# An attention kernel with routed experts: where weight quarters are loaded, and when the first transposes are copied

## The chip, the cores and the metric

The kernel runs on one core of one Trainium2 chip. That core has five instruction streams that work side by side: TensorE (PE, with its weight loads PEld), VectorE (DVE), ScalarE (ACT), GpSimd (POOL) and SyncE (SP). POOL and SP issue the DMAs here. The metric is the time of one execution in microseconds on the device, as the median of several runs.

## The reference

Attention over 8 sequences of 576 tokens with 8 heads of 64, with a position bias that is the same for all sequences, and then one of 8 expert networks for each token:

```python
scores = scale * np.matmul(q, k.transpose(0, 1, 3, 2))
x = (np.log1p(np.abs(rel)) / psi_i)[..., None]
bias = np.maximum(x @ w1 + b1, 0.0) @ w2
scores = scores + bias.transpose(2, 0, 1)[None]
attn = softmax(scores)
attn_out = np.matmul(attn, v)                 # 8 x 8 x 576 x 64
x = attn_out as (4608 tokens, 512)
for e in range(8):
    mask = domain_id == e
    out[mask] = np.maximum(x[mask] @ w1[e], 0.0) @ w2[e]   # 512 -> 1024 -> 512
```

## The kernel before

**Bias.** `_phase_bias` computes the bias once, in nine blocks `ib` of positions. `hidden` makes 16 rows `hr` for a block on VectorE (L202) and ScalarE (L199); `outputs` multiplies them on TensorE in three groups (chunks 0 and 1, chunks 2 and 3, chunk 4), each into one of three score buffers of the ring `G.ring()`. ScalarE writes exp(bias) from there (L234, L237, L244), and for chunk 3 VectorE also takes a raw copy from the same buffer (`biasW`, L241). `hidden(ib + 1)` is issued ahead of `outputs(ib)`. The bias code is a generator: it stops at each `yield`, and `run` calls it again at chosen units (`LAST_ROWS`), so that the three groups of block 8 lie between the first scores.

**Attention.** `_Attention.run` goes through the sequences b = 0 to 7 in an order written out by hand (`ROUND`). A unit such as `m01` is the scores of head pair 0 and key chunk 1: two matmuls (L532) into a ring buffer, and an exp on ScalarE (L560, tile `e`). `r` units are for the 64 last keys, `l` and `x` for the 64 last queries. `W` multiplies with the bias on VectorE (L571), `A` is attention times values on TensorE (L584, L588) into the one accumulator `G.acc()` (tile `pu`), `N` divides by the sums on VectorE (L614, L615). `T` transposes q and k of the next sequence on TensorE (L476), `D` copies them from PSUM (`take`, L501, L506, tile `qkT`). Sequence 0 has no round before it, so `_phase_bias` transposes and copies it: pairs (0, 1) and (2, 3) both go through the accumulator. The fourth head pair's attention of a sequence, and its last queries, are finished in the next round, so a sequence's finished rows are scattered by POOL to `fire_x` in DRAM one round later (L645: four scatters `xt`, one `xl`), sorted by expert.

**Weights.** Each expert has four quarters (two of w1, two of w2), 32 in all, each 512 KB when landed. `G.w.load(n, home)` issues the next n of them on POOL's queue. Homes are twelve tiles of `wsb` (`G.w_first`), the six rotating tiles `n4` that q, k and v are loaded through, and fourteen tiles of `wsb2` (`G.w_late`) in the expert phase. `late(b, ui)` runs after each unit (ui is the unit's number, `m00` is 1, `r1` is 9, `m20` is 10, `m23` is 13). `_Issue` keeps POOL's DMAs in the order in which they are written; scatters of one permutation are free among themselves.

**Experts.** At unit r1 of sequence 7, SP issues `xA`, a transposing DMA of the first 512 rows of expert 0 (sequences 0 to 6 fill them; L952). `_phase_moe` runs `first_early` on xA (L809), two `second` blocks (L775), `first_rest` on the last 128 rows (L817), which `fetch` transposes once sequence 7 is scattered (L788, tile `xT`), and three more `second` blocks. Experts 1 to 7 follow with `first` (L799) and five `second`. Each `second` is copied to one of eight tiles `res` (L778), scattered to the output by POOL with indices `ids` (L779, L790), and followed on POOL's queue by one weight quarter (L737). A quarter in `w_late` beyond the fourteenth waits until TensorE has finished with the first of these tiles.

Of the kernel before, what the change touches and what calls it, by code (L numbers as in the profile page):

```python
# [10 lines left out]
F16 = mybir.dt.float16  # L11
# [19 lines left out]
NSLOT = E * CAP + 128 * NOVF  # L31
PAD = 1 << 20
LN_EXP = 6
XW = DM + 2


# [25 lines left out]
""".split()  # L62


LAST_ROWS = {"m01": 1, "m03": 1, "m11": 2}


def rap(t, off, dims, nparts=None):
# [47 lines left out]
def _setup_constants(tc, G, w1, b1, w2):  # L116
# [9 lines left out]
    nc.scalar.add_instruction(mybir.InstLoadActFuncSet(  # L126
        name=nc.get_next_instruction_name(), engine=mybir.EngineType.Activation, act_func_set_id=LN_EXP,
        ins=[], outs=[]))
# [55 lines left out]
def _phase_bias(tc, G, route, at, x_dram):  # L184


    nc = tc.nc
    fsb = G.bias_pools.enter_context(tc.tile_pool(name="fsb", bufs=1, side="right"))
    def hidden(ib, between=None):
        hrl = []  # L190
        for k16 in range(16):
            if ib < 8:
                r, a = ib // 2, 16 * (ib % 2) + k16
                m, c0 = 32 * r + a, C4 - (16 * a + r)
            else:
                m, c0 = 128 + k16, W4 + C1 - 4 * k16
            hr = fsb.tile([P, S], F16, tag="hr", name="hr", bufs=34)
            if k16 in ((2, 5, 8, 11, 14) if ib < 2 else (3, 8, 13) if ib % 2 == 0 else (5, 11)):
                nc.scalar.activation(out=hr, in_=G.L4[:, c0: c0 + S], func=AF.Relu,  # L199
                                     bias=G.pb1[:], scale=G.slope[:, m: m + 1])  # L200
            else:
                nc.vector.tensor_scalar(out=hr, in0=G.L4[:, c0: c0 + S],  # L202
                                        scalar1=G.slope[:, m: m + 1], scalar2=G.nb1[:],
                                        op0=AO.mult, op1=AO.max)
            hrl.append(hr)
            if (ib, k16) == (0, 7):
                G.slopes(16, NGR)
            if (ib, k16) in ((1, 1), (1, 5), (1, 9), (2, 1), (2, 5)):
                next(route)
            if between is not None and k16 == between[0]:  # L210
                at.take(0, between[1])
        return hrl

    def outputs(ib, hrl):
        for jcs in ((0, 1), (2, 3), (4,)):
            eb = G.ring()
            for k16 in range(16):
                for lj, jc in enumerate(jcs):
                    hr = hrl[k16]
                    if jc < 4:  # L220
                        nc.tensor.matmul(out=eb[:, lj, 32 * k16: 32 * k16 + 32],  # L221
                                         lhsT=rap(hr, jc, [[4, 128]]),
                                         rhs=G.W2BIG[:, 0:32], start=True, stop=True)
                    else:
                        nc.tensor.matmul(out=eb[0:64, lj, 32 * k16: 32 * k16 + 32],
                                         lhsT=hr[:, 512:576],
                                         rhs=G.W2BIG[:, 0:32], start=True, stop=True)
            ebv = eb.rearrange("p l (i h) -> p l h i", h=8)
            i0 = 64 * ib
            if jcs[0] == 4:  # L230
                for h2 in range(2):
                    o = G.biasR[64 * h2: 64 * h2 + 64, :, i0: i0 + 64] if ib < 8 else \
                        G.biasRL[64 * h2: 64 * h2 + 64]
                    nc.scalar.activation(out=o, in_=ebv[0:64, 0, h2::2, :],  # L234
                                         func=AF.Exp, bias=0.0, scale=0.125)
            elif ib < 8:
                nc.scalar.activation(out=G.biasM[:, jcs[0]: jcs[0] + 2, :, i0: i0 + 64], in_=ebv,  # L237
                                     func=AF.Exp, bias=0.0, scale=0.125)
                for lj, jc in enumerate(jcs):
                    if jc in RAW:  # L240
                        nc.vector.tensor_copy(out=G.biasW[jc][:, :, i0: i0 + 64], in_=ebv[:, lj, RAW[jc]:, :])  # L241
            else:
                for lj in range(2):
                    nc.scalar.activation(  # L244
                        out=G.biasL[:, jcs[0] // 2, lj, :, :, :].rearrange("p h q i -> p q h i"),
                        in_=ebv[:, lj, :, :].rearrange("p (q h) i -> p q h i", h=2),
                        func=AF.Exp, bias=0.0, scale=0.125)
            yield

    hrl = hidden(0)  # L250
    for ib in range(9):
        after = hidden(ib + 1, {6: (3, (4,)), 7: (9, (0, 1))}.get(ib)) if ib < 8 else None
        if ib == 1:
            nc.vector.memset(G.zero.rearrange("p o (r d) -> p (o r) d", r=4)[:, :, DM:].bitcast(I32), PAD)
            nc.sync.dma_start(out=x_dram.rearrange("(p c r) d -> p c (r d)", p=P, r=4),
                              in_=G.zero.to_broadcast([P, NSLOT // P // 4, 4 * XW]))
        for _ in outputs(ib, hrl):
            if ib == 8:
                yield
        if ib == 0:  # L260
            next(route)
        if ib in (5, 6, 7):
            ps = {5: (4,), 6: (0, 1), 7: (2, 3)}[ib]
            at.transposes(0, ps, G.acc())
        if ib == 7:
            yield
        hrl = after
# [143 lines left out]
class _Attention:  # L411
# [85 lines left out]
    def take(self, b, ps):  # L497
        asb = self.G.asb
        if ps == (4,):
            t = self.qkTl[b] = asb.tile([P, 4, 2, 128], F16, tag="qkTl", name="qkTl", bufs=2)  # L500
            self.nc.vector.tensor_copy(out=t, in_=self.pt.pop((b, 4)))  # L501
        else:
            t = asb.tile([P, 2, 2, 512], F16, tag="qkT", name="qkT", bufs=4)
            for i, p in enumerate(ps):
                self.qkT[b, p] = t[:, i]
            self.nc.vector.tensor_copy(out=t.rearrange("p i x f -> p i (x f)"),  # L506
                                       in_=self.pt.pop((b, ps)).bitcast(F16))

    def scores(self, b, u):
        nc, G = self.nc, self.G  # L510
# [146 lines left out]
            self.load_vrag(b)  # L657

    def run(self, bias, route, late):
        units = [("r", 0)] + [("m", p, c) for p in (0, 1) for c in range(4)] + [("r", 1)] + \  # L660
                [("m", 2, c) for c in range(4)] + [("l", 0), ("l", 1), ("x",)] + \
                [("m", 3, c) for c in range(4)]
# [7 lines left out]
        def unit(b, name):  # L670
            if b >= B:
                return
            ui = names[name]
            jobs[b, name] = self.scores(b, units[ui])
            if b == 0 and name in LAST_ROWS:
                for _ in range(LAST_ROWS[name]):
                    next(bias, None)
            if (b, name) == (0, "m00"):
                self.take(0, (2, 3))
            if b == 0 and ui > 2:  # L680
                for _ in range(2):
                    next(route, None)
            if b < B - 2 and ui == 3:
                self.load_qk(b + 2)
            if b < B - 2 and ui == 5:
                self.load_v(b + 2)
                self.load_last(b + 2)
            if b < B - 2 and ui == 7:
                self.load_vrag(b + 2)
            late(b, ui)  # L690
# [76 lines left out]
def _phase_moe(tc, G, moe_w1, moe_w2, x_dram, out):  # L767
# [50 lines left out]
                                 rhs=xT[:, dc, EARLY:], start=(dc == 0), stop=(dc == 3))  # L818
        nc.scalar.activation(out=hT[:, :, EARLY:], in_=hps, func=AF.Relu, bias=0.0, scale=1.0)

    G.w.load(2, G.n4)
    G.w.load(2, G.w_late)
    xTs = {e: fetch(e) for e in range(2)}
    novf = None
    for e in range(E):
# [11 lines left out]
        else:  # L837
            for fc in range(8):
                nc.scalar.activation(out=hT[:, fc, :].rearrange("p (a b) -> p a b", a=2),  # L839
                                     in_=first(e, xT, ((fc, 0), (fc, 1))),  # L840
# [47 lines left out]
def kernel(  # L888
# [14 lines left out]
    G = _Ctx()  # L903
# [9 lines left out]
    with tc.manual_schedule(engines={ET.PE, ET.DVE, ET.Activation}):  # L913
        with ExitStack() as att:
# [20 lines left out]
            at = _Attention(tc, G, q, k, v, x_dram)  # L935
            at.start()
            bias = _phase_bias(tc, G, route, at, x_dram)
            def late(b, ui):
                if (b, ui) == (0, 7):
                    assert next(bias, None) is None  # L940
                    G.bias_pools.close()
                    wsb = ctx.enter_context(tc.tile_pool(name="wsb", bufs=1, side="right", reuse_waits="tile"))
                    G.w_first = lambda name: wsb.tile([P, 2048], F16, tag="w", name=name, bufs=12)
                if b < 6 and ui == 10:
                    G.w.load(1, G.w_first)
                if (b, ui) in ((6, 1), (7, 5)):
                    G.w.load(3, G.w_first)
                if (b, ui) == (6, 3):
                    G.w.load(3, G.n4)
                if (b, ui) == (B - 1, 9):  # L950
                    G.early = G.n4("xA").rearrange("p (c t) -> p c t", c=4)
                    nc.sync.dma_start_transpose(out=G.early, in_=x_dram[0: EARLY, 0:DM])  # L952
# [36 lines left out]
```

## Time and profile before

| | us |
|---|---|
| median of 3 runs (397.8 to 398.48) | 398.47 |
| the profiled execution's own time | 398.14 |
| its span, first to last instruction | 396.6 |
| PE, ACT, DVE, POOL busy in the span | 324.9, 246.9, 236.6, 182.5 |
| bias alone, until the first exp of scores | 0 to 54.8 |
| attention, until the last attention matmul | 54.8 to 222.5 |
| experts | 222.5 to 396.6 |

The rows further down are read so. A timeline row has the start, the duration in us, engine, line, operation, output<-input with shape, the number of merged instructions, and in brackets the idle time of that engine before the row and what ended it. A window row has the stretch, its length, the busy time of PE, PEld, DVE, ACT and POOL with instruction counts, then the share of TensorE's full clock that was granted, the mean busy share of the 16 DMA engines (over 1 when packets of two queues overlap) and what they moved.

### The profile page before, as it was taken

To read this page: it belongs to the slowest core of one execution; us is meant where nothing else is said; L and a number is where in the kernel's file an instruction comes from. 1 tells how busy PE (TensorE), PEld (TensorE's weight loads), DVE (VectorE), ACT (ScalarE), POOL (GpSimd) and SP (SyncE) were. 2 spreads that over 40 slices of the span, in tenths; PEclk is the share of its full clock that TensorE was granted. 3 is DMA by queue.
4 is the path that set the end of the run, shared out by engine and by line. 5 is a ranking of instruction groups with operands and counts; after the bars stand their busy time and mean duration, and the time that the engine had idled before them with its cause. 6 is when DMAs were issued, how large, how long until landed. Compare 5 with 4: busy or idle time off the path is not lost.

```text
span 396.6 us, 9316 instructions
## 1 busy us (share of the span) xinstructions
PE 324.9 (82%) x3938; PEld 214.2 (54%) x3938; DVE 236.6 (60%) x440; ACT 246.9 (62%) x302; POOL 182.5 (46%) x220
## 2 busy tenths in 40 slices
PE   1599968789898989898787493999969985999893
PEld 1477846656566666565555243555536542656551
DVE  7999986999999999999889400212211202031211
ACT  8999968699999999999899040333214220514230
POOL 9250033049696969696445070836410046040312
PEclk9999988899999999999999697999989998999997
DMA  5999999039999999999966959999999259130302
GB/s 90 176 189 367 373 263 182 4 38 170 133 165 135 163 140 164 132 167 135 199 139 123 132 108 186 192 201 228 227 216 222 56 83 276 40 116 5 126 26 96
DMA packets 90996, 61.30 MB, mean 155 GB/s; under 512 B 43462, under 2 KB 85190, under 8 KB 90953
## 3 DMA queue, kind: packets, MB, share of 16 engines
q0 software_dynamic: 59904, 45.12, 69.2%
q1 hardware_dynamic: 31048, 15.57, 17.5%
q8 instruction: 31, 0.51, 0.5%
q14 instruction: 13, 0.10, 0.1%
HBM read 61.93 MB, written 24.70 MB: 218 GB/s over the span
## 4 chain that ended last, share of the span: by engine, by line
issue 24%; DVE 21%; DMA 19%; ACT 15%; PE 12%; POOL 6%; SPq 1%; POOLq 1%; DVEq 0%
ACT e L560 14%; DVE hr L202 7%; DMA out_dram<-res,ids 7%; DVE e L571 6%; POOL out_dram L779 5%; PE pu L588 4%; DMA w<-in_moe_w_dram 4%; DMA xA<-fire_x 3%; DMA ids<-fire_x 3%; DVE xt L615 2%; PE sc L532 2%; DVE qkT L506 2%; PE sc L476 2%; PE sc L538 1%; PE pu L584 1%
## 5 line engine op out<-in xcount | busy, mean ns | idle before, releaser
L560 ACT ACTIVATE e<-sc 128x1024 f16<-128x1024 f32 x168 | 152.2, 1019 | 13.1 <-PE sc L532 5.6
L778 DVE COPY res<-ops 128x512 f32<-128x512 f32 x40 | 27.6, 691 | 137.9 <-PE ops L775 126.8
L839 ACT ACTIVATE hT<-hps 128x640 f16<-128x640 f32 x56 | 39.4, 703 | 93.2 <-PE hps L799 76.1
L775 PE MATMUL ops<-w,hT 128*128 128x512 f16 x320 | 72.9, 387 | 5.3 <-DVE res L778 5.3
L571 DVE TENSOR_TENSOR e<-e,biasM 128x2048 f16<-128x2048 f16 x64 | 72.9, 1150 | 0.6 <-ACT e L560 0.4
L779 POOL DMA_INDIRECT out_dram<-res,ids x40 | 40.5, 1012 | 68.5 <-DVE res L778 48.7
L799 PE MATMUL hps<-xT,w 128*128 128x320 f16 x448 | 63.7, 304 | 5.3 <-DMA xT<-fire_x 4.3
L799 PEld LDWEIGHTS <-w 128*128 128x128 f16 x448 | 44.2, 99 | 25.2 <-issue 5.7
L532 PE MATMUL sc<-qkT 64*128 64x512 f16 x256 | 45.1, 385 | 15.0 <-ACT e L560 13.8
L775 PEld LDWEIGHTS <-hT 128*128 128x128 f16 x320 | 31.8, 100 | 43.6 <-issue 8.5
L645 POOL DMA_INDIRECT fire_x<-xt,posi x32 | 46.6, 1457 | 12.0 <-issue 8.2
L588 PE MATMUL pu<-vext,e 128*128 128x65 f16 x1024 | 48.1, 196 | 4.0 <-DVE e L571 4.0
L588 PEld LDWEIGHTS <-e 128*128 128x128 f16 x1024 | 43.4, 99 | 6.9 <-DVE e L571 5.0
L737 POOL DMA_DIRECT2D w<-in_moe_w_dram x32 | 27.7, 943 | 37.6 <-PE hps L799 32.2
L202 DVE TENSOR_SCALAR hr<-L,slope,nb 128x576 f16<-128x576 f16 x116 | 41.5, 427 | 0.0
L221 PE MATMUL sc<-W2BIG,hr 128*128 128x32 f16 x576 | 27.7, 193 | 13.1 <-DVE hr L202 9.6
L645 POOL DMA_INDIRECT fire_x<-xl,posi x8 | 10.4, 1296 | 52.8 <-DVE e L571 40.3
L221 PEld LDWEIGHTS <-hr 128*128 128x128 f16 x576 | 23.2, 116 | 17.8 <-DVE hr L202 14.1
L532 PEld LDWEIGHTS <-qkT 64*128 64x128 f16 x256 | 12.2, 93 | 35.5 <-issue 29.2
L584 PE MATMUL pu<-vrag,e 128*128 128x130 f16 x128 | 28.6, 223 | 2.2 <-DVE xl L631 1.4
L615 DVE TENSOR_TENSOR xt<-pu,rz 128x512 f16<-128x512 f32 (+1 forms) x33 | 22.3, 675 | 1.5
L199 ACT ACTIVATE hr<-L,pb,slope 128x576 f16<-128x576 f16 x28 | 22.2, 858 | 1.0 <-DVE slope L165 0.8
(128 smaller groups left out, 365.9 us busy)
## 6 DMA issues: line engine op xcount, KB each, us to landing
w<-in_moe_w_dram POOLq DMA_DIRECT2D x32, 512.0 KB
fire_x<-zero SPq DMA_DIRECT2D x1, 9252.0 KB
qn<-in_q_dram POOLq DMA_DIRECT2D x8, 512.0 KB
kn<-in_k_dram POOLq DMA_DIRECT2D x8, 512.0 KB
vst<-in_v_dram POOLq DMA_DIRECT2D x8, 512.0 KB
out_dram<-res,ids POOLq DMA_INDIRECT x40
last<-zero SPq DMA_DIRECT2D x2, 256.0 KB
last<-in_q_dram POOLq DMA_DIRECT2D x16, 32.0 KB
```

Of the source, the lines that this page charges most:

```text
L202: nc.vector.tensor_scalar(out=hr, in0=G.L4[:, c0: c0 + S], scalar1=G.slope[:, m: m + 1], scalar2=G.nb1[:], op0=AO.mult, op1=AO.max)
L221: nc.tensor.matmul(out=eb[:, lj, 32 * k16: 32 * k16 + 32], lhsT=rap(hr, jc, [[4, 128]]), rhs=G.W2BIG[:, 0:32], start=True, stop=True)
L532: mm(out=sc[:, h2, :], lhsT=self.qkT[b, p][hs[h2], 1, 128 * c: 128 * c + 128], rhs=self.qkT[b, p][hs[h2], 0, :], start=not raw, stop=True)
L560: nc.scalar.activation(out=ef[:, 0:n], in_=sf[:, 0:n], func=AF.Exp, bias=0.0, scale=0.125)
L571: self.nc.vector.tensor_tensor(out=job[0], in0=job[0], in1=job[1], op=AO.mult)
L584: mm(out=self.pu[:, c // 2, o: o + 130], lhsT=er[:, p % 2, 128 * c: 128 * c + 128], rhs=vr[:, p, :], start=True, stop=False, skip_group_ch ...
L588: mm(out=self.pu[:, c // 2, o + 65 * h2: o + 65 * h2 + 65], lhsT=self.e[b, ("m", p, j)][:, h2, 128 * c: 128 * c + 128], rhs=vx[:, 2 * p + ...
L645: inst = self.nc.gpsimd.indirect_dma_start(out=self.x_dram[:, :], out_offset=bass.IndirectOffsetOnAxis(ap=self.G.posi[0:n, c:c + 1], axis= ...
L775: nc.tensor.matmul(out=ops_, lhsT=hT[:, fc, t0: t0 + 128], rhs=G.w.w2(e, fc), start=(fc == 0), stop=(fc == 7))
L779: inst = nc.gpsimd.indirect_dma_start(out=out[:], out_offset=bass.IndirectOffsetOnAxis(ap=idx.bitcast(I32), axis=0), in_=res[:], in_offset ...
L799: nc.tensor.matmul(out=hps[:, i, 0:HC], lhsT=G.w.w1(e, dc, fc), rhs=xT[:, dc, HC * hf: HC * hf + HC], start=(dc == 0), stop=(dc == 3))
L839: nc.scalar.activation(out=hT[:, fc, :].rearrange("p (a b) -> p a b", a=2), in_=first(e, xT, ((fc, 0), (fc, 1))), func=AF.Relu, bias=0.0, ...
```

## The change

Five edits:

- The last two `yield`ed pieces of the bias move: the copy of sequence 0's pairs (0, 1) comes after row 1 of `hidden(8)` instead of row 9; the transposes and the copy of its pairs (2, 3) move out of `_phase_bias` to unit m01; the three groups of block 8 follow units m03, m10 and m11 instead of m01, m03 and m11.
- The copy of sequence 1's pairs (2, 3) goes from VectorE to ScalarE.
- Sequences 0 to 6 load 4, 2, 1, 2, 1, 1, 1 quarters at unit m20; before, sequences 0 to 5 loaded one each.
- Sequence 6 loads three quarters into `n4` at m02, and two more at m23. Before it loaded three into `wsb` and three into `n4`, and sequence 7 three into `wsb` at m10. So 17 quarters instead of 15 stand ahead of the expert phase, and none in sequence 7.
- The four quarters at the head of `_phase_moe` are gone; the other 15 follow one to each `second`, as before.

```diff
+W_FIRST = {0: 4, 1: 2, 2: 1, 3: 2, 4: 1, 5: 1, 6: 1}
-LAST_ROWS = {"m01": 1, "m03": 1, "m11": 2}
+LAST_ROWS = {"m03": 1, "m10": 1, "m11": 2}
@@ _phase_bias
-        after = hidden(ib + 1, {6: (3, (4,)), 7: (9, (0, 1))}.get(ib)) if ib < 8 else None
+        after = hidden(ib + 1, {6: (3, (4,)), 7: (1, (0, 1))}.get(ib)) if ib < 8 else None
...
-        if ib in (5, 6, 7):
-            ps = {5: (4,), 6: (0, 1), 7: (2, 3)}[ib]
-            at.transposes(0, ps, G.acc())
+        if ib in (5, 6):
+            at.transposes(0, (4,) if ib == 5 else (0, 1), G.acc())
@@ take
-            self.nc.vector.tensor_copy(out=t.rearrange("p i x f -> p i (x f)"),
-                                       in_=self.pt.pop((b, ps)).bitcast(F16))
+            o, i = t.rearrange("p i x f -> p i (x f)"), self.pt.pop((b, ps)).bitcast(F16)
+            if (b, ps) == (1, (2, 3)):
+                self.nc.scalar.copy(out=o, in_=i)
+            else:
+                self.nc.vector.tensor_copy(out=o, in_=i)
@@ run
-            if (b, name) == (0, "m00"):
+            if (b, name) == (0, "m01"):
+                self.transposes(0, (2, 3), G.acc())
                 self.take(0, (2, 3))
@@ _phase_moe
-    G.w.load(2, G.n4)
-    G.w.load(2, G.w_late)
@@ late
-                if b < 6 and ui == 10:
-                    G.w.load(1, G.w_first)
-                if (b, ui) in ((6, 1), (7, 5)):
-                    G.w.load(3, G.w_first)
-                if (b, ui) == (6, 3):
-                    G.w.load(3, G.n4)
+                if ui == 10 and b in W_FIRST:
+                    G.w.load(W_FIRST[b], G.w_first)
+                if (b, ui) in ((6, 3), (6, 13)):
+                    G.w.load(3 if ui == 3 else 2, G.n4)
```

POOL's queue from the last four scatters of sequence 6 to the second output scatter, before (`fire_x<-` are the scatters of sequences 6 and 7, `w` the quarters, `out_dram` the output):

```order
L645 DMA fire_x<-xt,posi 9216x514 x4
L737 DMA w_4362<-in_moe_w_dram 128x4x512
L737 DMA w_4364<-in_moe_w_dram 128x4x512
L737 DMA w_4366<-in_moe_w_dram 128x4x512
L639 IOTA xt 128x4
L639 IOTA xl 64x1
L645 DMA fire_x<-xl,posi 9216x514
L645 DMA fire_x<-xt,posi 9216x514 x4
L737 DMA w_4677<-in_moe_w_dram 128x4x512
L737 DMA w_4679<-in_moe_w_dram 128x4x512
L737 DMA w_4681<-in_moe_w_dram 128x4x512
L737 DMA w_4683<-in_moe_w_dram 128x4x512
```

The same place now, from the last scatter of sequence 6:

```order
L648 DMA fire_x<-xt,posi 9216x514 x4
L642 IOTA xt 128x4
L642 IOTA xl 64x1
L648 DMA fire_x<-xl,posi 9216x514
L648 DMA fire_x<-xt,posi 9216x514 x4
L784 DMA out_dram<-res,ids 4608x512
L742 DMA w_4758<-in_moe_w_dram 128x4x512
L784 DMA out_dram<-res,ids 4608x512
```

The three quarters behind sequence 6's scatters and the four behind sequence 7's are gone; the first quarter now stands behind the first output scatter.

VectorE's queue from the rows of bias block 8 to the first bias product, before (`biasW` is the raw copy of block 7, the first `qkT` is pairs (0, 1) of sequence 0, the second pairs (2, 3)):

```order
L202 TENSOR_SCALAR hr<-L_110,slope,nb_120 128x576 x8
L506 COPY qkT<-pu 128x2048
L202 TENSOR_SCALAR hr<-L_110,slope,nb_120 128x576 x5
L241 CAST biasW_73<-sc 128x2x64
L506 COPY qkT<-pu 128x2048
L571 TENSOR_TENSOR e<-e,biasR 128x1024
```

And now:

```order
L203 TENSOR_SCALAR hr<-L_110,slope,nb_120 128x576 x2
L510 COPY qkT<-pu 128x2048
L203 TENSOR_SCALAR hr<-L_110,slope,nb_120 128x576 x11
L242 CAST biasW_73<-sc 128x2x64
L510 COPY qkT<-pu 128x2048
L574 TENSOR_TENSOR e<-e,biasR 128x1024
```

The first copy stands six rows earlier; the cast still stands behind all thirteen rows, and the second copy still behind the cast.

## Rows read from the trace of the kernel before

**Rows 1.** Windows, a stretch of steady attention.

```profile
100.00:125.00 25.00, 21.53 (x372) 15.18 (x371) 24.27 (x37) 24.42 (x28) 18.00 (x20) 1.00 1.12 148
```

**Rows 2.** Timeline of PE, end of attention and the experts.

```profile
221.89 0.60 PE L588 MATMUL pu<-vext,e 128*128 128x65 f16 x8
226.10 8.36 PE L809 MATMUL hps<-xA,w 128*128 128x512 f16 x32 [3.61 <-DMA xA<-fire_x]
...
244.55 3.60 PE L817 MATMUL hps<-xT,w 128*128 128x128 f16 x32 [6.63 <-DMA xT<-fire_x]
...
253.76 8.86 PE L799 MATMUL hps<-xT,w 128*128 128x320 f16 x64
262.45 8.80 PE L775 MATMUL ops<-w,hT 128*128 128x512 f16 x40
271.81 8.85 PE L799 MATMUL hps<-xT,w 128*128 128x320 f16 x64 [0.56 <-DMA xT<-fire_x]
...
293.01 10.53 PE L799 MATMUL hps<-xT,w 128*128 128x320 f16 x64 [3.71 <-DMA xT<-fire_x]
...
331.32 5.20 PE L775 MATMUL ops<-w,hT 128*128 128x512 f16 x16 [5.28 <-DVE res L778]
336.36 8.86 PE L799 MATMUL hps<-xT,w 128*128 128x320 f16 x64
```

**Rows 3.** Timeline of SP, issue of the transposing DMAs.

```profile
213.29 8.26 SPq L952 DMA_TRANSPOSE xA<-fire_x  x1
234.65 1.87 SPq L788 DMA_TRANSPOSE xT<-fire_x  x1
...
249.89 10.84 SPq L788 DMA_TRANSPOSE xT<-fire_x  x1
```

**Rows 4.** Timeline of POOL, scatters and weight quarters.

```profile
211.44 2.69 POOL L737 DMA_DIRECT2D w<-in_moe_w_dram  x3
...
226.88 0.95 POOL L645 DMA_INDIRECT fire_x<-xl,posi  x1 [12.49 <-DMA xA<-fire_x]
...
232.02 0.97 POOL L645 DMA_INDIRECT fire_x<-xt,posi  x1 [0.30 <-issue]
232.99 3.44 POOL L737 DMA_DIRECT2D w<-in_moe_w_dram  x4
248.62 1.07 POOL L779 DMA_INDIRECT out_dram<-res,ids  x1 [12.19 <-DMA ids<-fire_x]
...
321.17 0.76 POOL L737 DMA_DIRECT2D w<-in_moe_w_dram  x1 [32.19 <-PE hps L799]
```

**Rows 5.** Windows with the granted clock and the DMA traffic.

```profile
70.00:84.00 14.00, 11.16 (x161) 8.22 (x160) 13.76 (x23) 10.41 (x13) 0.08 (x1) 0.88 0.00 1
104.00:123.50 19.50, 17.12 (x303) 12.03 (x300) 18.94 (x28) 18.94 (x22) 15.29 (x18) 1.00 1.09 152
222.00:226.00 4.00, 0.49 (x9) 0.38 (x7) 2.13 (x8) 0.00 (x0) 0.00 (x0) 0.50 1.10 176
244.00:248.00 4.00, 3.45 (x33) 3.46 (x34) 0.00 (x0) 0.00 (x0) 0.00 (x0) 0.50 1.42 205
306.00:308.00 2.00, 2.00 (x11) 0.94 (x10) 0.69 (x1) 0.00 (x0) 0.00 (x0) 1.00 1.08 214
```

**Rows 6.** Timeline of DVE, start and end of attention.

```profile
53.50 0.28 DVE L241 CAST biasW<-sc 128x128 f16<-128x128 f32 x1
...
64.42 1.22 DVE L506 COPY qkT<-sc 128x2048 f16<-128x2048 f16 x1 [2.64 <-PE sc L476]
...
222.75 0.42 DVE L615 TENSOR_TENSOR xt<-pu,rz 128x256 f16<-128x256 f32 x1
```

**Rows 7.** Timeline of ACT, first sequence and sequence 6.

```profile
54.84 2.85 ACT L560 ACTIVATE e<-sc 128x1024 f16<-128x1024 f32 x3 [3.89 <-PE sc L538]
...
74.33 1.02 ACT L560 ACTIVATE e<-sc 128x1024 f16<-128x1024 f32 x1 [2.85 <-PE sc L545]
...
191.62 8.83 ACT L560 ACTIVATE e<-sc 128x1024 f16<-128x1024 f32 x10 [1.64 <-PE sc L532]
```

More of the change, by code (lines that the diff above doesn't have):

```diff
@@ L659, in run @@
     def run(self, bias, route, late):
+        G = self.G
         units = [("r", 0)] + [("m", p, c) for p in (0, 1) for c in range(4)] + [("r", 1)] + \
```

## The prediction, made before the changed kernel ran

> **What bounds the kernel now.** First the busy times in windows. In steady attention ScalarE works 24.42 of 25 us [rows 1], so a round of about 19.5 us is ScalarE's, and TensorE, VectorE and the DMAs have a little room. Then the timeline of TensorE from the end of attention on, since there ScalarE is no longer the bound: the reader is to see five gaps in brackets, 3.61, 6.63, 0.56, 3.71 and 5.28 us [rows 2], 19.8 us in all. The first four end with a transposing DMA (xA, xT), the fifth with a result copy. Then SP and POOL, to see what those DMAs stood beside. xA is issued at 213.29 [rows 3], just behind three weight quarters issued from 211.44 on [rows 4], and lets TensorE go on only at 226.10 [rows 2], 12.8 us later. The scatters of sequence 7 wait for xA to have read fire_x (12.49 us idle on POOL), four quarters are issued behind them from 232.99 on [rows 4], and the first xT, issued at 234.65 [rows 3], shares the DMA engines with these and is there at 244.55 [rows 2], 9.9 us later for 128 rows. Without weights in flight the transposes are fast: in 306 to 308, while POOL waits with the quarter that it issues at 321.17, 214 GB/s are moved [rows 4, 5], so 640 rows of 1 KB (655 KB) take about 3.1 us and xA's 512 rows about 2.5 us, plus start and completion. For these I take 2.6 us, what the last scatter needs from its issue at 232.02 to the release of xT at 234.65 [rows 3, 4].
>
> **The change part by part.**
>
> (a) *First sequence.* ScalarE idles 3.89 us before its first exp at 54.84 [rows 7]. The first copy moves ahead of six rows, and r0 no longer stands behind the transposes, so r0's exp can start near 51. But m00 needs the score buffer of block 7's second group, which VectorE releases with the cast at 53.50 to 53.78 [rows 6], and that stays behind the same 13 rows. So m00's exp starts near 54.3; before it followed r0's exp, 54.84 plus one third of 2.85, near 55.8: 1.5 us won. The 32 transposes now between m01 and m02 give half a microsecond back. By the copy at 64.42 about 0.8 us is left, all inside its 2.64 us of idle time [rows 6]. The copy given to ScalarE is 2048 columns, at most twice the 1.02 us of a 1024-column exp, and falls into the 2.85 us that ScalarE idles before 74.33 [rows 7], while VectorE, which is what that idle time waited for by way of TensorE, loses 1.2 us of work [rows 6]. I take -1.0. Bounds: -3.9, if all of ScalarE's first gap went; +1.5, since the copy of pairs (2, 3) now stands at the head of VectorE's queue until near 56.3 with every bias product behind it, 2.4 us later than the cast lets it start, of which the moved copy gives back about 1.
>
> (b) *Quarters in sequences 0 to 6.* Three more in sequence 0 meet DMA engines that are idle from 70 to 84 (1 GB/s) [rows 5]: nothing. One more in sequences 1 and 3 is 512 KB at about 200 GB/s (205 in the window 244 to 248 [rows 5]), 2.6 us of a round of 19.5 whose DMA share is 1.09 where full stretches show 1.4 [rows 5]: there is room for it, and the q, k and v loads behind it have a round's time. Cost 0; 2.6 each if there is no room. Sequence 6 issues six as before, but three of them later, and no longer all six ahead of its scatters; ScalarE's gap of 1.64 us there [rows 7] may go or stay: 0, bounds -1.6 and +1.6. The Trainium skill's page "DMA: Bandwidth & Descriptors", section "Issuing engines are not separate DMA queues", says that DMAs of all issuing engines run on the same 16 DMA engines and interleave; by it the seven quarters beside the transposes are not removed but laid beside the loads of earlier rounds, and the question is only whether these rounds have room, as just priced. The trace agrees as far as it goes: with weights in flight xT takes 21 us instead of about 3.
>
> (c) *xA.* Without the three quarters xA takes 2.5 + 2.6 = 5.1 us from 212.3 (213.29 less a), so it lands at 217.4, while attention's last matmul ends at 222.49 [rows 2]. So the 3.61 us gap goes, with 5 us of cover: -3.6. If xA were slower than that it would cost only beyond 222.
>
> (d) *Clock.* In 222 to 226 the granted clock was 0.50, the 1.2 GHz level, after TensorE had thinned out; first_early's 32 matmuls took 8.36 us [rows 2, 5]. At full clock 40 such take 8.80 [rows 2], so 32 take 7.0: -1.4, 0 if the clock falls all the same. The Trainium skill ("TensorE: Matmul & The Clock Gate", section "What's actually happening") holds that throttled is the default state and activity releases it; by that rule a TensorE that goes on without a gap keeps 2.4 GHz, but one that is thinly used at the end of attention may lose it even without a gap, and then this -1.4 is 0.
>
> (e) *first_rest.* The scatters of sequence 7 no longer wait for xA. With (a), the first half of the rows is normalised near 220.5, the second at 222.2 (223.17 less 1) [rows 6]; four scatters at 1.27 us each [rows 4] and 2.6 to landing give 227.2 for the issue of xT, before 234.65. With 128 rows it lands near 230.4; TensorE asks for it at 221.5 + 7.0 + 3.5 (16 matmuls) = 232.0. The 6.63 us gap goes: -6.6. first_rest itself ran at clock 0.50 [rows 5] in 3.60, and from its start to expert 1 it was 9.21 us (244.55 to 253.76) [rows 2]; at full clock 1.8 + 24 x 0.22 = 7.1: -2.1. Expert 1 starts at 253.76 - 1.0 - 3.6 - 1.4 - 6.6 - 2.1 = 239.1.
>
> (f) *Later xT.* Expert 1's xT goes out near 229.8, before any quarter, and is there near 235. Expert 2's is issued near 233.5, and from there on the quarters run beside it as before: from issue 249.89 to use 271.81 were 21.9 us, the next came 21.2 us later [rows 2, 3]. So they land at 255.4 and 276.6; TensorE, at 17.5 us an expert, asks at 256.6 and 274.1. Waits of 0.56 + 3.71 become about 2.5: -1.7. Expert 4's comes when the 14 quarters that are let through are nearly done: 0, bound +3.
>
> (g) *Result tiles.* The fifteenth late quarter waits on POOL for expert 4's first half (32.19 us) [rows 4], with output scatters queued behind it. Before, it stands behind expert 2's third block, so 2 + 5 = 7 of the 8 result tiles are stuck; now behind its fifth, so 5. Expert 4's five blocks then find three tiles and two PSUM buffers, and the 5.28 us gap goes. After it the clock was low: 16 matmuls took 5.20 instead of 3.5 [rows 2]. Together -7.0; 0 if the scatters land too late for this too.
>
> Sum: -1.0 - 3.6 - 1.4 - 6.6 - 2.1 - 1.7 - 7.0 = -23.4. The profiled execution took 398.14 (span 396.6 and 1.5 around it), so 374.7; against the median of 398.47, 0.3 above it, 375.
>
> **The rivals.**
>
> *The collision only moves on (20%).* The first quarter is issued about 2 us after expert 0's indices land, and expert 1's xT is then under way. If it is caught half done, it finishes at the shared pace, 21 us for a whole one, so some 10 us late, near 245 where 239 was wanted, and those behind it start later too: 6 at expert 1 and some 3 more up to expert 4, 375 + 9 = 384. For it: every 640-row transpose beside quarters took over 20 us. Against it: in the kernel before, expert 1 found its xT ready, though the first output scatter and quarter came at 248.62 [rows 4], 5 us before it.
>
> *Transposes are slow by themselves (9%).* Then xA takes its 12.8 us also alone and lands at 225, the first xT its 9.9, and c, d and e give nothing. Only a and g stay: 398.5 - 8.0 = 390.5. Against it stand the 214 GB/s of 306 to 308.
>
> *Attention becomes bound by the DMAs (5%), slower than before.* If the 1.09 in a round is already full, the backlog of the extra quarters never drains, and the q and k loads come late for the transposes of the next sequence: each of rounds 1 to 6 is stretched by 512 KB at 152 GB/s [rows 5], 3.4 us, 20 in all. The quarters of sequence 6 then still run when xA is issued, and c to e (13.7) are lost as well: 398.5 - 23.4 + 20 + 13.7 = 409. With c to e lost it decides from 9.7 / 6 = 1.6 us a round. Against it: rounds with a quarter have no wait for a load on TensorE's side, and the stretches at 1.4 show what the engines can take.
>
> **How the numbers follow.** The forecast, 375, has 66%; its own range is 369 (a and the gap in sequence 6 at their better ends, no wait at expert 3) to 380 (a at +1.5, the clock lost, expert 4 waiting). With the first rival it reaches to 386. I give 369 to 387, which leaves out the two others and some tails. About 0.2% (0.8 us) is what a measurement can tell from no change. Faster by more: 66 + 20 + 9 = 95, less 1 for ends that meet near nothing: 94%; the same 1%; slower 5%.
>
> **What would show it.** On TensorE's timeline: no gap before L814 (first_early) and its 32 matmuls near 7 us; first_rest without a gap, expert 1 near 239; a gap of 0 to 4 us at expert 3 and none inside expert 4's second half. On SP: xA issued near 212, the first xT near 227. On ScalarE: the first exp near 51, then a gap of some 2 us before the second. On POOL: the long wait of a quarter with two more output scatters ahead of it. I am wrong if xA still takes over 9 us, if expert 1 waits for its xT, or if a round of attention is longer than 20 us.

## The result, and the profile after

The changed kernel took 375.77 us in the median (370.67, 374.99, 376.56 and 378.19), against 398.13 (397.77 to 398.48) for the kernel before on the same chip: ratio 0.9364, 95% interval 0.927 to 0.9459. The ratio leaves out executions more than 1.5% above the fastest of their kernel, here two of the four; the median has all four, and the ratio of the two medians is 0.944. The forecast was 375, with 369 to 387 as its range. The profiled execution is the fastest one: 370.67 us, span 368.9, mean granted clock 0.983 (before: 398.14, 396.6, 0.956).

TensorE's timeline, to be read against [rows 2]:

```profile
218.17 0.23 PE L587 MATMUL pu<-vrag,e 128*128 128x130 f16 x1 [1.41 <-DVE xl L634]
...
219.71 0.27 PE L587 MATMUL pu<-vrag,e 128*128 128x130 f16 x1 [0.73 <-DVE xt L618]
...
220.32 0.65 PE L591 MATMUL pu<-vext,e 128*128 128x65 f16 x8
220.78 8.14 PE L814 MATMUL hps<-xA,w 128*128 128x512 f16 x32
228.76 3.62 PE L780 MATMUL ops<-w,hT 128*128 128x512 f16 x16
232.21 1.95 PE L822 MATMUL hps<-xT,w 128*128 128x128 f16 x32
234.00 5.34 PE L780 MATMUL ops<-w,hT 128*128 128x512 f16 x24
239.18 8.86 PE L804 MATMUL hps<-xT,w 128*128 128x320 f16 x64
...
256.50 8.86 PE L804 MATMUL hps<-xT,w 128*128 128x320 f16 x64
...
273.83 8.86 PE L804 MATMUL hps<-xT,w 128*128 128x320 f16 x64
...
325.81 8.86 PE L804 MATMUL hps<-xT,w 128*128 128x320 f16 x64
334.50 8.80 PE L780 MATMUL ops<-w,hT 128*128 128x512 f16 x40
344.34 8.85 PE L804 MATMUL hps<-xT,w 128*128 128x320 f16 x64 [1.04 <-DVEq L832]
```

All five brackets of before are gone; the two ahead of first_early are the last matmuls of attention waiting for VectorE. Expert 1 starts at 239.18, and experts 1 to 5 follow one another every 17.3 us. The 1.04 us at the end were there before too (at 372.21).

SP's queue, with the issues of [rows 3]:

```profile
210.76 1.95 SPq L953 DMA_TRANSPOSE xA<-fire_x  x1
226.54 1.19 SPq L793 DMA_TRANSPOSE xT<-fire_x  x1
...
228.41 2.63 SPq L793 DMA_TRANSPOSE xT<-fire_x  x1
...
231.69 3.22 SPq L793 DMA_TRANSPOSE xT<-fire_x  x1
...
235.66 14.09 SPq L793 DMA_TRANSPOSE xT<-fire_x  x1
```

And POOL's, with those of [rows 4]:

```profile
218.88 0.92 POOL L648 DMA_INDIRECT fire_x<-xl,posi  x1 [9.60 <-DVE xl L634]
...
231.65 1.00 POOL L784 DMA_INDIRECT out_dram<-res,ids  x1 [6.74 <-DVE res L783]
232.61 1.01 POOL L742 DMA_DIRECT2D w<-in_moe_w_dram  x1
...
300.31 0.79 POOL L742 DMA_DIRECT2D w<-in_moe_w_dram  x1 [18.83 <-PE hps L804]
```

xA's issue takes 1.95 us where it took 8.26, from issue to landing it takes 4.5 us for 12.8, and the scatters wait for VectorE's rows, no longer for xA. The first xT goes out 8 us earlier. The order to remember is on the two queues together: expert 2's xT is issued at 231.69, and the first late quarter 0.9 us behind it, at 232.61. A quarter still waits long on POOL (18.83), but no matmul waits for a result copy any more.

Windows, columns as in [rows 5]:

```profile
70.00:84.00 14.00, 11.57 (x177) 8.80 (x175) 12.98 (x22) 12.71 (x14) 1.45 (x3) 0.88 0.82 132
104.00:123.50 19.50, 17.13 (x302) 12.04 (x298) 18.94 (x28) 18.94 (x22) 15.30 (x17) 1.00 1.26 177
218.00:222.00 4.00, 3.10 (x39) 2.22 (x40) 1.65 (x7) 0.00 (x0) 2.51 (x3) 0.69 0.17 50
222.00:226.00 4.00, 4.00 (x18) 1.76 (x17) 1.20 (x5) 1.52 (x2) 2.31 (x3) 0.88 0.28 100
```

The idle stretch 70 to 84 now carries quarters (132 GB/s for 1), and a round with an extra quarter has a DMA share of 1.26 for 1.09, yet VectorE and ScalarE are busy for the same 18.94 us. In 218 to 222 the granted clock is 0.69, at the thin end of attention with its idle times of 1.41 and 0.73 us; the eight matmuls at 220.32 already take 0.65 us where eight such at 218.55 took 0.42, so the clock fell before first_early began.

The first sequence, on ScalarE and then on VectorE:

```profile
51.26 1.02 ACT L563 ACTIVATE e<-sc 128x1024 f16<-128x1024 f32 x1 [0.20 <-PE sc L541]
54.51 1.94 ACT L563 ACTIVATE e<-sc 128x1024 f16<-128x1024 f32 x2 [2.23 <-PE sc L535]
...
98.02 18.97 ACT L563 ACTIVATE e<-sc 128x1024 f16<-128x1024 f32 x21 [0.50 <-PE sc L535]
```

```profile
53.54 0.28 DVE L242 CAST biasW<-sc 128x128 f16<-128x128 f32 x1
56.79 1.22 DVE L510 COPY qkT<-pu 128x2048 f16<-128x2048 f16 x1 [2.98 <-PE pu L476]
```

r0's exp starts at 51.26 and m00's waits for the cast at 53.54, as worked out; the copy at the head of VectorE's queue costs 2.98 us of its time. The round that began at 98.66 before begins at 98.02.

Where the time went, with first_early's start and expert 1's start on TensorE as marks (each figure a difference of timeline rows and the span; "from 1" and "longer execution" are experiments below):

| | before | forecast | after | after, longer execution | from 1 |
|---|---|---|---|---|---|
| start of first_early | 226.10 | 221.5 | 220.78 | 219.85 | 220.78 |
| from there to expert 1 | 27.66 | 17.6 | 18.40 | 17.32 | 17.32 |
| from expert 1 to the end | 142.84 | 134.1 | 129.72 | 137.43 | 129.50 |
| span | 396.6 | 373.2 | 368.9 | 374.6 | 367.6 |

### The profile page after: what moved, and what is told of

Same layout as the page of the kernel before. It is cut to its first block, busy times and chain, and to the rows that moved or that the text cites. A ratio compares the mean times of both kernels' runs of the same rounds, so it can differ in the third digit from the quotient of the medians.

```text
span 368.9 us, 9308 instructions
## 1 busy us (share of the span) xinstructions
PE 319.6 (87%) x3938; PEld 211.9 (57%) x3938; DVE 235.5 (64%) x439; ACT 249.4 (68%) x303; POOL 181.6 (49%) x220
## 5 line engine op out<-in xcount | busy, mean ns | idle before, releaser
L780 PE MATMUL ops<-w,hT 128*128 128x512 f16 x320 | 70.5, 379 | 0.0
L804 PE MATMUL hps<-xT,w 128*128 128x320 f16 x448 | 62.0, 299 | 1.0 <-DVEq L832 1.0
L535 PE MATMUL sc<-qkT 64*128 64x512 f16 x256 | 46.0, 395 | 16.7 <-ACT e L563 13.4
L648 POOL DMA_INDIRECT fire_x<-xt,posi x32 | 45.7, 1428 | 11.0 <-issue 9.1
L446 POOL DMA_DIRECT2D qn<-in_q_dram x8 | 7.6, 950 | 31.1 <-PE pu L476 31.1
```

Of the source, the lines that this page charges most:

```text
L535: mm(out=sc[:, h2, :], lhsT=self.qkT[b, p][hs[h2], 1, 128 * c: 128 * c + 128], rhs=self.qkT[b, p][hs[h2], 0, :], start=not raw, stop=True)
L648: inst = self.nc.gpsimd.indirect_dma_start(out=self.x_dram[:, :], out_offset=bass.IndirectOffsetOnAxis(ap=self.G.posi[0:n, c:c + 1], axis= ...
L780: nc.tensor.matmul(out=ops_, lhsT=hT[:, fc, t0: t0 + 128], rhs=G.w.w2(e, fc), start=(fc == 0), stop=(fc == 7))
L804: nc.tensor.matmul(out=hps[:, i, 0:HC], lhsT=G.w.w1(e, dc, fc), rhs=xT[:, dc, HC * hf: HC * hf + HC], start=(dc == 0), stop=(dc == 3))
```

## The experiments

Twelve runs, in three groups of four. Kernels of a group ran on one chip, and each group on another, on which the kernel before took 397.54, 400.49 and 398.55 us; ratios are always to the kernel before on the same chip.

**1. The changed kernel again.** No edit.

> The changed kernel as it is, once more, since its four executions lay between 370.7 and 378.2 us where those before lay within 0.7. Theory 'race': expert 2's transposed rows are issued within about 2 us of expert 0's first weight quarters, and it depends on the execution how much of them passes before the quarters; a longer execution then shows a gap of 2 to 6 us of TensorE behind an xT at expert 2, 3 or 4. Theory 'clock': a longer execution has no such gap, but a lower granted clock over stretches of the experts, and every matmul there takes longer. Expected: median 373 to 377, again spread over 4 us or more.

374.94 us in the median, 370.64 to 378.6: ratio 0.9426 (0.939 to 0.9463). The spread is real; the profiled execution was again a short one, with the order of the two queues as above (expert 2's xT at 231.34, the first quarter at 232.54).

**2. Late quarters from expert 1 on.** The 15 late quarters no longer follow expert 0's blocks.

```diff
-            G.w.load(1, G.w_late)
+            if e >= 1:
+                G.w.load(1, G.w_late)
```

> The changed kernel, with the 15 late quarters behind the blocks of experts 1 to 3 instead of 0 to 2, so that expert 1's, 2's and 3's xT go out with no quarter beside them. Theory 'race': the spread goes, all executions near 370 (369 to 372, within 1.5 us), some 4 us under the changed kernel's median; no gap at experts 1 to 4. Theory 'clock': the same spread and median as the changed kernel in the same job.

369.41 us, 367.37 to 369.52: ratio 0.9273 (0.9249 to 0.9297). Faster than both kernels, and the spread is down from 8 us to 2.

**3. Three quarters back in sequence 7, ahead of xA.**

```diff
-W_FIRST = {0: 4, 1: 2, 2: 1, 3: 2, 4: 1, 5: 1, 6: 1}
+W_FIRST = {0: 4, 1: 2, 2: 1, 3: 2, 4: 1, 5: 1}
...
-                if (b, ui) in ((6, 3), (6, 13)):
-                    G.w.load(3 if ui == 3 else 2, G.n4)
+                if (b, ui) == (6, 3):
+                    G.w.load(3, G.n4)
+                if (b, ui) == (7, 5):
+                    G.w.load(1, G.w_first)
+                    G.w.load(2, G.n4)
```

> The changed kernel, with the last three of its 17 early quarters moved from sequence 6 back to sequence 7, ahead of xA. Theory 'collision' (a transpose is slow because it shares the DMA engines with quarters): xA takes 10 to 13 us again instead of about 4, TensorE waits some 3 us for it and starts at the low clock, sequence 7's scatters wait for xA, but the first xT meets no quarter; expert 1 starts 3 to 4 us later than in the changed kernel, so +3.5 us (2 to 6). Theory 'slow by itself' or 'hidden anyway': xA and the time as in the changed kernel, 0.

375.84 us, 374.06 to 390.45, three of the seven above 382. Its median is 0.9 above that of experiment 1, its lowest time 3.4: where +3.5 was expected, the time decides nothing. The profiled execution is the longest. In it SP and then TensorE show

```profile
210.91 9.89 SPq L956 DMA_TRANSPOSE xA<-fire_x  x1
234.36 1.19 SPq L793 DMA_TRANSPOSE xT<-fire_x  x1
```

```profile
225.87 10.02 PE L814 MATMUL hps<-xA,w 128*128 128x512 f16 x32 [5.02 <-DMA xA<-fire_x]
```

Beside quarters xA's issue is long again, it lands 14.9 us after its issue instead of 4.5, and TensorE waits for it. That supports term (c), by one execution; what the shorter ones met is not shown.

**4. Four quarters back at the head of the experts.**

```diff
+    G.w.load(2, G.n4)
+    G.w.load(2, G.w_late)
...
-            G.w.load(1, G.w_late)
+            if (e, kk) >= (0, 2):
+                G.w.load(1, G.w_late)
...
-                if (b, ui) in ((6, 3), (6, 13)):
-                    G.w.load(3 if ui == 3 else 2, G.n4)
+                if (b, ui) == (6, 3):
+                    G.w.load(3, G.n4)
```

> The changed kernel, with two quarters of sequence 6 and the first two late ones issued at the head of the experts, four in a row behind sequence 7's scatters, as in the kernel before; the other 13 follow from expert 0's third block on, so the last one stands where it does in the changed kernel. Theory 'collision': the first xT lands near 236 instead of 229, first_rest waits about 4 us and runs at the low clock (another 2.5), expert 1 starts about 6 us later, and the later xT run beside quarters for longer, another 0 to 5: +9 us (6 to 12). Theory 'hidden anyway': TensorE has work until 232 and the four are through by then, under +2 us.

377.61 us, 376.38 to 378.18: ratio 0.95 (0.948 to 0.9519). SP and TensorE:

```profile
226.17 1.28 SPq L793 DMA_TRANSPOSE xT<-fire_x  x1
...
228.18 12.86 SPq L793 DMA_TRANSPOSE xT<-fire_x  x1
```

```profile
236.48 3.32 PE L822 MATMUL hps<-xT,w 128*128 128x128 f16 x32 [4.35 <-DMA xT<-fire_x]
...
245.09 8.86 PE L804 MATMUL hps<-xT,w 128*128 128x320 f16 x64
```

A wait of 4.35 us, of the 6.63 of before, and the slow first_rest come back, and expert 1 starts at 245.09, 5.9 us later than in the first profile: that much of term (e) is these four quarters; the rest goes with the first xT's earlier issue (226.17 for 234.65). No later xT is late, and the median is 2.7 us above that of experiment 1, the lowest time 5.7: less than expected.

**5. The bias part alone, on the kernel before.** The edits of `_phase_bias`, `take`, `run` and `LAST_ROWS`, none of the weights.

> The kernel before, with the bias part of the change alone (three bias groups one unit later, transposes and copy of sequence 0's pairs 2 and 3 at m01, one copy on ScalarE); all quarters as before. The changed kernel's rounds begin 0.65 us earlier (98.02 for 98.66 on ScalarE). Theory 'lead kept': that is kept to the end, -0.65 us (0 to -1.5). Rival 'taken back': xA, the first xT and the scatters set when the experts start, and the lead is lost, 0 or slightly slower. ScalarE's gap of 1.64 us in sequence 6 stays if the six quarters ahead of the scatters make it, and goes if it had to do with the first sequence's order.

399.28 us, ratio 0.9968 (0.9939 to 0.9998): 1.2 us less than before, hardly clear of no change. In its profile the rounds run 2.2 us ahead of those in the profile of before, which is from another chip (96.45 for 98.66); but the granted clock from 60 to 79 was 1.00 here and 0.83 and 0.81 there, so the lead is not the edit's alone. Expert 3 starts at 292.15 after a wait of 3.88, 0.9 us ahead, a wait of 1.55 for ScalarE follows in expert 5, and the span is 396.6 again. In this profile the lead is lost to late xT and that wait; the times fit a lead that is kept as well.

**6. The late quarters two blocks later, on the kernel before.** The four at the head stay; the fifteenth then stands behind two more output scatters.

```diff
-            G.w.load(1, G.w_late)
+            if (e, kk) >= (0, 2):
+                G.w.load(1, G.w_late)
```

> The kernel before, with its 13 late quarters behind blocks 2 to 14 of the experts instead of 0 to 12, so that the one that waits for expert 4's first half has five result tiles stuck behind it instead of seven; everything else as before. Theory 'result tiles': the gap of 5.28 us in expert 4 and the low clock after it go, -7.0 us (5 to 8), perhaps 1 more from fewer quarters beside the first xT. Rival 'scatters too late': the wait moves to a later block of expert 4 and stays over 3 us; -2 or less.

390.2 us, ratio 0.9717 (0.9674 to 0.9761): 10.3 faster. The first two gaps stay (4.00 and 5.88), those at experts 2 and 3 go, and TensorE no longer waits for a result copy; inside expert 5 it waits twice for ScalarE instead:

```profile
328.75 1.25 PE L799 MATMUL hps<-xT,w 128*128 128x320 f16 x8 [1.58 <-ACT hT L839]
331.62 5.80 PE L799 MATMUL hps<-xT,w 128*128 128x320 f16 x32 [1.62 <-ACT hT L839]
```

So two blocks are enough for (g), and they also clear the way for the xT of experts 2 and 3 (the issue of expert 2's takes 3.40 us for 10.84 before): (f) lies in the start of the late quarters. This goes with a gain above the 7 to 8 us expected.

**7 and 8. "From expert 1 on", with the bias part undone, and with only the copy of sequence 1's pairs (2, 3) back on VectorE.**

```diff
-            if (b, ps) == (1, (2, 3)):
+            if False:
```

> The changed kernel with the late quarters from expert 1 on (as in e3_from1), with the bias part of the change undone. Theory 'two separate gains': 0.65 us slower than e3_from1 (0 to 1.5), so about 370, and ScalarE has no gap in sequence 6. Rival 'the quarters need the earlier start': over 2 us slower.

> As e3_from1, with the copy of sequence 1's pairs 2 and 3 back on VectorE. Theory 'the moved copy carries the bias part': VectorE's bias products of sequence 0 come 1.1 us later, the wait of attention-times-values grows by as much, and the time by 0.5 to 1.2 us, so that without it the bias part wins nothing. Rival 'ScalarE's gap closes elsewhere': under 0.3 us.

376.53 us (ratio 0.9399, 0.9369 to 0.9429) and 375.44 (0.9374, 0.9345 to 0.9403): 4 to 5 us worse against before than experiment 2, for edits worth 1.2 in experiment 5. The rows of 8 show short stalls of TensorE inside the transposes of a sequence, for no reason that the profile has, and ScalarE waits for them:

```profile
90.80 0.35 PE L476 MATMUL sc<-idn,kn 128*64 128x128 f16 x5 [0.37 <-issue]
91.55 0.25 PE L476 MATMUL sc<-idn,kn 128*64 128x128 f16 x2 [0.39 <-issue]
```

```profile
90.88 1.94 ACT L563 ACTIVATE e<-sc 128x1024 f16<-128x1024 f32 x2 [1.55 <-PE sc L476]
```

Either the order of these edits keeps such stalls away, or the chip had them. The last group tells.

**9 to 12. Experiments 2, 7, 8 and the changed kernel, word for word, side by side on a third chip.**

> The version that begins the late quarters with expert 1's blocks, again, as the anchor for the two kernels beside it. Both theories: ratio to the kernel before 0.927, within 0.925 to 0.932; first_early 220.8 us after the span's start with no wait, expert 1 near 238, no later wait of TensorE over 0.5 us. If its ratio comes near 0.938 here, the 5 us of the other two lay in the chip and not in their order.

> The same version with the bias part of the change undone, beside it on one chip. Theory 'two separate gains' (a, the head of the first sequence, worth what the trace of after showed): 0.65 us slower than the anchor, 0.3 to 1.5, the rounds of scores 0.65 us later. Rival 'the stalls depend on the order': 5 to 6 us slower, with the idle time of ScalarE spread over the first and the sixth sequence, where TensorE's transposes stand idle between issues.

> The same version with one edit of the bias part undone: the copy of the second sequence's transposes of pairs 2 and 3 stands on VectorE again. Theory 'two separate gains': 0 to 1 us slower than the anchor. Rival 'the stalls depend on the order': 5 to 6 us slower, short stalls of TensorE in the transposes and ScalarE gaps of 1 to 2 us behind score units in the second and the seventh sequence.

> The changed kernel again, beside the anchor. Theory 'race' (the late quarters of expert 0's blocks compete with the transposed loads for experts 1 to 3): 4 to 6 us slower than the anchor in the median with a spread of 5 us or more, its fastest execution within 3 us of the anchor. Rival 'the chip alone': no wider spread than the anchor's and within 2 us of it.

| | median | lowest and highest | ratio |
|---|---|---|---|
| from 1 | 369.34 | 368.36 to 369.46 | 0.929 (0.9248 to 0.9332) |
| from 1, bias part undone | 370.64 | 369.6 to 371.68 | 0.9329 (0.9284 to 0.9375) |
| from 1, copy on VectorE | 369.74 | 368.53 to 370.7 | 0.9296 (0.9251 to 0.934) |
| changed kernel | 375.58 | 368.88 to 376.37 | none |

The rival falls: undoing the bias part costs 1.3 us (no overlap of the executions), the copy 0.4 (within the noise). The same two kernels were 5.7 to 5.9 us longer on the second chip. In the profiles the difference lies ahead of the experts: first_early starts at 226.47 and 224.95 there, at 221.47 and 220.97 here. So the order of these edits does not cause the stalls by itself. What does stays open: on the second chip the kernel before was only 2 us longer, and the changed kernel itself was not run there.

This time the profile of the changed kernel fell on a long execution, 376.37. TensorE, SP and POOL:

```profile
217.68 0.23 PE L587 MATMUL pu<-vrag,e 128*128 128x130 f16 x1 [1.41 <-DVE xl L634]
...
219.22 0.22 PE L587 MATMUL pu<-vrag,e 128*128 128x130 f16 x1 [0.73 <-DVE xt L618]
...
219.85 7.07 PE L814 MATMUL hps<-xA,w 128*128 128x512 f16 x32
...
237.17 8.86 PE L804 MATMUL hps<-xT,w 128*128 128x320 f16 x64
...
255.92 8.87 PE L804 MATMUL hps<-xT,w 128*128 128x320 f16 x64 [1.26 <-DMA xT<-fire_x]
...
276.78 11.61 PE L804 MATMUL hps<-xT,w 128*128 128x320 f16 x64 [3.35 <-DMA xT<-fire_x]
```

```profile
228.03 3.38 SPq L793 DMA_TRANSPOSE xT<-fire_x  x1
...
232.07 12.58 SPq L793 DMA_TRANSPOSE xT<-fire_x  x1
...
245.43 20.09 SPq L793 DMA_TRANSPOSE xT<-fire_x  x1
```

```profile
230.32 1.00 POOL L784 DMA_INDIRECT out_dram<-res,ids  x1 [5.68 <-DMA ids<-fire_x]
231.29 1.00 POOL L742 DMA_DIRECT2D w<-in_moe_w_dram  x1
```

Here the first quarter is issued at 231.29, 0.8 us ahead of expert 2's xT (232.07); in the two shorter profiled executions it came 0.9 and 1.2 us behind. That xT's issue takes 12.58 us instead of 3.22, and it lands 23.8 us after its issue instead of 7.7; expert 3's stands behind it on SP and goes out at 245.43 instead of 235.66. Experts 2 and 3 wait 1.26 and 3.35, and the matmuls of expert 3 are slow (11.61 for 8.86). Two shifts put the quarter ahead. On POOL it came 1.3 us earlier: first_early ran at full clock, 7.07 us, so its result was ready before the indices, and POOL waited only for these; in the first profile POOL waited for the result until 231.65. On SP expert 2's xT came 0.4 us later, because the issue of expert 1's took 3.38 us instead of 2.63. So this execution wins 1.1 us at first_early and loses 7.4 at experts 2 and 3.

The other profiles agree on what the order does. Where the first late quarter goes out ahead of expert 2's xT (before by 0.2 us, experiment 5 by 0.5, experiment 3 by 1.1), the issue of that xT takes 10.8 to 11.5 us and TensorE waits for late xT; where an edit puts the quarter 2.4 to 2.5 us behind it (experiments 4 and 6), the issue takes 3.3 to 3.4 us and no later xT is late. Starting the late quarters with expert 1 takes the race away, on SP:

```profile
229.00 3.18 SPq L793 DMA_TRANSPOSE xT<-fire_x  x1
...
232.85 4.15 SPq L793 DMA_TRANSPOSE xT<-fire_x  x1
...
237.72 3.74 SPq L793 DMA_TRANSPOSE xT<-fire_x  x1
```

and on TensorE no expert waits for its xT any more:

```profile
220.78 7.07 PE L814 MATMUL hps<-xA,w 128*128 128x512 f16 x32
...
272.75 8.86 PE L804 MATMUL hps<-xT,w 128*128 128x320 f16 x64
```

Of the 16 executions of the changed kernel 4 took 372.5 us or less, 12 between 374.06 and 378.6; one of the twelve was profiled. The gain of "from 1" over it, 6.2 us here and 5.5 on the first chip, is what the race costs in the median. That the clock of first_early decides the order is seen in three profiles of one kernel, not forced by an edit; in experiment 3 the quarter was ahead although first_early was slow (10.02 us), because xA and with it every xT was late.

## Why the prediction was right

The sum was -23.4, and the time 375.0 for a median of 375.77. By its steps:

- **(a) First sequence, -1.0.** The order of events was as told: r0 early, m00 behind the cast, the copy at the head of VectorE's queue. The trace gives -0.64 at the second round, and undoing the part costs 1.3 (experiment 10). Right.
- **(b) Quarters in sequences 0 to 6, 0.** Rounds start every 19.5 us still (98.02, 117.53), so the room was there. The 1.64 us gap of sequence 6, left open at ±1.6, went: with (a) the start of first_early gains 1.7 beyond (c). It belongs to the quarters: ScalarE keeps a gap of 0.95 there in experiment 5, with the old order of the quarters, and has none in experiment 10, without the bias part.
- **(c) xA, -3.6.** Right: xA lands 4.5 us after its issue for a forecast of 5.1, first_early follows attention without a gap, and it waits again in the profile with quarters beside xA (experiment 3).
- **(d) Clock of first_early, -1.4.** In the first profile only -0.2 (8.14 for 8.36): first_early followed without a wait, and the clock was at 0.69 all the same. In the long execution and in "from 1" it was 7.07, the forecast value, in experiment 11 again 8.06. The Trainium skill ("TensorE: Matmul & The Clock Gate", section "What's actually happening") has the low clock as the default that activity releases; the trace agrees in that the clock fell behind TensorE's idle times at the end of attention. The rows do not tell why the clock fell in one execution and not in another, with the same idle times of 1.41 and 0.73 us ahead of first_early in both.
- **(e) first_rest, -6.6 and -2.1.** Right: 1.95 us at full clock, no wait. Expert 1 at 239.18 for a forecast of 239.1 is in part luck: first_early began 0.7 us earlier than forecast and took 1.1 longer. Experiment 4 brings 5.9 us of the loss back with the four quarters alone.
- **(f) Later xT, -1.7.** This is the term that was mis-sized, in both directions. The step reads "Expert 2's is issued near 233.5, and from there on the quarters run beside it as before". In the long execution that is what happened: the forecast had the xT of experts 2 and 3 land at 255.4 and 276.6, and the experts that waited for them began at 255.92 and 276.78. Its waits and slow matmuls add up to 7.4 us for 5.9 before, +1.4. In the short ones expert 2's xT goes out ahead of the first quarter, no expert waits, and the term is -5.9. The forecast took one number for a race of about 1 us between two queues. That the median fits 375 is in part luck: the first profile's span is 4.3 us under the forecast 373.2, the long one's 1.4 above it, three of the four executions of the result were long ones by their times, and the 1.1 us of (b) were not counted.
- **(g) Result tiles, -7.0.** Right: 5.28 of gap and 1.7 of slow clock gone in every profile of the changed kernel; in experiment 6 the shift alone takes the wait for result copies away.

Of the rivals, "transposes are slow by themselves" falls with xA landing in 4.5 us instead of 12.8, and "bound by the DMAs" with the 19.5 us rounds. "The collision only moves on" was half true: not at expert 1, where it was placed, but at experts 2 and 3, and not in every execution. What was said for it, that every 640-row transpose beside quarters took over 20 us, was not so: before, expert 1's was issued at 237.25 and in use at 253.76 without a wait. The Trainium skill's page "DMA: Bandwidth & Descriptors", section "Issuing engines are not separate DMA queues", says that DMAs of all issuers interleave on the same engines; the trace agrees: the same xT issue takes 3.22 or 12.58 us, by which side of it the first quarter falls.

## What to carry to other kernels

Bulk loads should begin behind the last latency-bound transfer that somebody waits for, not behind an instruction on another queue that is usually later: read the issue times of both queues, and where they lie within a microsecond of each other, expect two outcomes and look at the spread, not the median alone. One profile shows one of them, and here the first was of the rarer kind. Whether a shorter phase upstream pays while the transfer behind it is still late is not settled: the bias part was worth 1.2 us with the late xT (experiment 5) and 1.3 without (experiments 9 and 10), though in the profile of experiment 5 its lead is lost.

## What was not expected of the hardware

- The granted clock fell ahead of first_early in some executions (first_early 8.14 us, window 218 to 222 at 0.69) and not in others (7.07, at 1.00), with the same kernel and the same waits ahead of it.
- Whether a weight quarter is issued 0.8 us ahead of a transposing DMA or 0.9 us behind it goes with 12.58 or 3.22 us for that DMA's issue, and with some 6 us of the kernel.
- Two kernels, each run word for word on two chips, took 370.64 and 369.74 us on one and 376.53 and 375.44 on the other, while the kernel before differed by 2 (398.55 and 400.49). On the slower chip TensorE stood still for 0.4 us at a time between transposes, with nothing in the profile that it waited for.
